# Gate logits through VectorE block transposes and a block-diagonal gate, for batches 3 to 7

## The chip, the cores and the metric

The kernel runs on one core of a Trainium2 chip. The metric is the device time of one execution in microseconds. All arrays are float32.

## The reference

An FFT filter over the sequence is followed by a mixture of experts in which every token goes to the one expert with the largest gate logit.

```python
# x: (8, 2496, 256); filter: (1249, 256) complex
X = np.fft.rfft(x, axis=1)
y = np.fft.irfft(X * (filt_r + 1j * filt_i)[None], n=2496, axis=1)   # (8, 2496, 256)

x = y.reshape(19968, 256)
logits = x @ w_gate                       # w_gate (256, 8)
expert_idx = np.argmax(logits, axis=1)
probs = np.exp(logits - logits.max(-1, keepdims=True))
probs /= probs.sum(-1, keepdims=True) + 1e-09
gate_w = probs[np.arange(N), expert_idx]
for e in range(8):                        # the tokens of each expert
    h = np.maximum(x[of_e] @ w1[e], 0.0)  # w1[e] (256, 1024)
    out[of_e] = gate_w[of_e, None] * (h @ w2[e])   # w2[e] (1024, 256)
```

## The kernel before

**The transform.** The length 2496 is 39 x 64, and the FFT is done as matmuls in four stages for each of the 8 batches. `stage_a` multiplies by a 39-point table, three blocks of 39 tokens at a time (117 partitions, TP). `stage_b` multiplies by a 64-point table, and VectorE applies the filter. `stage_c` is the 64-point inverse, and `stage_d` the 39-point inverse; its result `yo` holds y with tokens on the partitions (117 of them) and four columns of 256 features a tile. Between the stages the data goes through HBM (`zd`, `ud`). A batch has 22 such columns (NG), in six chunks (`CH`): five of four columns and one of two.

**The logits.** The gate needs features on the partitions. `turn_y` (L475) turns a chunk of y with TensorE transposes, 117x128 at a time, four for each pair of columns (L482), and copies the result from PSUM to `yt` with VectorE or ScalarE (`evac`, L234). `logits` (L488) takes four pairs at once and multiplies them by the gate matrix `wg`, padded to 32 columns: each pair writes 32 partitions of the PSUM tile `lt`, and so uses its own strip of 32 output columns of TensorE's array (L496). `turn_logits` (L502) copies `lt` to `ls`, transposes it back (L507) and stores it in `lg`, tokens on the partitions and 8 logits a token. A batch has three such groups, of 8, 8 and 6 columns.

**The routing.** `route` (L515), one call a group, finds the largest logit, the expert and the gate weight on VectorE. It ranks the tokens of each expert with two matmuls of the one-hot matrix `oe` by a triangle and by ones (`rk`, L554 and L555), which ScalarE copies to `pos` and `tot` (L557 to L559); VectorE scans and adds (L568 to L574) and writes `row`, the place of each token's row. GpSimd then appends the token's number and its gate weight `sd` to the rows of `yo` (L582, L586) and scatters them to HBM, one DMA for each column (L615).

**The experts.** The rows of each expert are read back in tiles of 512, 256 or 128, transposed on VectorE in blocks of 32x32 (`turn_x`, L748), and multiplied by w1 (L791 by a method with fewer products, or L832) and w2 (L849). The results are scattered to the output (L855).

**The order.** Nothing is ordered by the hardware's own choice: the program writes out each engine's queue by a small planner. `slot(k)` lists FFT steps with a due time within a slot, a cost, what they wait for and the stream they belong to: stage b and c of batch k, stage a of batch k+1, and stage d, logits and routing of batch k-1. The main loop takes the next step or, if a load is late (`late_in`), the first ready step of another stream (`other`), and mixes in expert steps by a credit. `now` is the planner's clock, `free` its belief of when VectorE ("v"), ScalarE ("s") and GpSimd ("p") are done. Routing runs as a generator in `side`, which can yield "wait" until the planner's clock has passed a due time. Tiles `yo` have 6 buffers (YB), `yt` 4.

Of the kernel before, what the change touches and what calls it, by code (L numbers as in the profile page):

```python
# [10 lines left out]
F32 = mybir.dt.float32  # L11
# [27 lines left out]
FT = F // P  # L39

# [13 lines left out]
def dft_tables():  # L54

    w = 2.0 * np.pi  # L60
    q = np.arange(N1)
    t = np.arange(N2)

    ta = np.zeros((NB, N1, NB, NS))
    td = np.zeros((NB, NS, NB, N1))
    for f in range(NF):
        ang = w * ((q * f) % N1) / N1
        for j in range(NB):
            ta[j, :, j, f] = np.cos(ang)
            td[j, f, j] = (2.0 if f else 1.0) / S * np.cos(ang)  # L70
            if f:
                ta[j, :, j, NF + f] = -np.sin(ang)
                td[j, NF + f, j] = -2.0 / S * np.sin(ang)

    ang = w * ((t[:, None] * t[None, :]) % N2) / N2
    c, sn = np.cos(ang), np.sin(ang)
    tb = np.block([[c, -sn], [sn, c]])
    tc = np.block([[c, sn], [-sn, c]])

    ids = np.zeros((NB, N1, NG))  # L80
    valid = np.zeros((NB, N1, NG))
    for j in range(NB):
        for i in range(len(range(j, N2, NB))):
            ids[j, :, i] = token(q, NB * i + j)
            valid[j, :, i] = 1.0


    sg = np.where(coefficients() <= S // 2, 1.0, -1.0)

    return {  # L90
        "ta": ta.reshape(TP, TK),
        "tb": tb,
        "tc": tc,
        "td": td.reshape(TK, TP),
        "sg": np.concatenate([sg[:, :NF // 2], sg[:, NF // 2:]]),
        "ids": ids.reshape(TP, NG),
        "valid": valid.reshape(TP, NG),
    }
# [22 lines left out]
def kernel(  # L121
# [52 lines left out]
    tau0 = perm.tile([1, 64], F32, name="tau0")  # L174
# [12 lines left out]
    tds = cst.tile([TK, TP], F32, name="tds")  # L187
# [4 lines left out]
    CT = 32  # L192
    wg = cst.tile([P, DH, CT], F32, name="wg")
    tri = cst.tile([TP, TP], F32, name="tri")
    ones = cst.tile([TP, P], F32, name="ones")
# [6 lines left out]
    vld = cst.tile([TP, NG], F32, name="vld")  # L202
    e_i = cst.tile([P, E], I32, name="e_i")
# [4 lines left out]
    tau_i = pro.tile([1, 64], I32, name="tau_i", bufs=1)  # L208
# [57 lines left out]
    def load_rest():  # L266
        nc.sync.dma_start(out=tds, in_=td)
        nc.vector.memset(wg, 0.0)
        nc.sync.dma_start(out=wg[:, :, :E], in_=moe_w_gate.rearrange("(i p) e -> p i e", p=P))
        nc.sync.dma_start(out=ids0, in_=ids)  # L270
        nc.sync.dma_start(out=vld, in_=valid)

    def make_constants():
        make_identity(nc, ident)
        nc.gpsimd.memset(ones, 1.0)
        nc.gpsimd.affine_select(
            out=tri, in_=ones[:, :TP], compare_op=ALU.is_gt, fill=0.0, base=0, pattern=[[1, TP]], channel_multiplier=-1
        )
        nc.gpsimd.memset(seg, 1.0)
        nc.gpsimd.memset(seg[:, :, 0:1], 0.0)  # L280
        nc.gpsimd.memset(tot, 0.0)
        nc.gpsimd.iota(prow, pattern=[[0, 1]], base=0, channel_multiplier=1)
        nc.gpsimd.iota(tau_i, pattern=[[1, 64]], base=0, channel_multiplier=0)
        nc.vector.tensor_copy(tau0, tau_i)
        nc.gpsimd.iota(e_i, pattern=[[1, E]], base=0, channel_multiplier=0)
        nc.vector.tensor_scalar(em8, in0=e_i, scalar1=-float(E), scalar2=None, op0=ALU.add)
        nc.vector.tensor_scalar(eoff, in0=e_i, scalar1=float(TE), scalar2=None, op0=ALU.mult)
        nc.vector.tensor_copy(cnt, eoff)
        nc.vector.tensor_copy(done, eoff[0:1, :])
        nc.vector.memset(one, 1.0)  # L290
# [106 lines left out]
    def stage_d(b, c):  # L397
        if c == 0:
            lgs[b] = sb.tile([TP, NG, E], F32, tag="lg", name="lg")
        i0, n = CH[c]  # L400
        held_y[0] += 1
        ui = outs.pop(("ui", c)) if b == 0 else ins.pop(("u", b, c))
        yo = outs["o", b, c] = sb.tile([P, 4, DR], F32, tag="y", name="yo", bufs=YB)[:TP]
        for j in range(0, n, 2):
            p = bank()
            if i0 + j + 2 < NG:
                mm(p[:TP, :], lhsT=tds, rhs=ui[:TK, j:j + 2, :], start=True, stop=True)
            else:

                for i, k in enumerate((TK, NS)):  # L410
                    mm(p[:TP, i * D:(i + 1) * D], lhsT=tds[:k, :], rhs=ui[:k, j + i, :], start=True, stop=True)
            evac(yo[:, j:j + 2, :D], p[:TP, :].rearrange("p (i d) -> p i d", i=2), 512)
# [63 lines left out]
    def turn_y(b, c):  # L476
        yo = outs["o", b, c]
        for j in range(0, CH[c][1], 2):
            pt = bank().rearrange("p (i q) -> p i q", i=4)
            for i in range(2):  # L480
                for dh in range(DH):
                    nc.tensor.transpose(  # L482
                        pt[:, 2 * i + dh, :TP], yo[:, j + i, dh * P:(dh + 1) * P], ident[:TP, :TP]
                    )
            yt = yts[b, c, j] = sb.tile([P, 4, TP], F32, tag="yt", name="yt", bufs=4)
            evac(yt, pt[:, :, :TP], 4 * TP)

    def logits(b, g):  # L488

        js = range(min(4, NG // 2 - 4 * g))  # L490
        w = len(js) * CT
        pair = [yts.pop((b, 2 * g + j // 2, 2 * (j % 2))).rearrange("p (i h) q -> p i h q", i=2) for j in js]
        lt = psr.tile([P, 2, E * NG], F32, tag="lt", name="lt")[:, :, :TP]
        for dh in range(DH):
            for j in js:
                mm(lt[j * CT:(j + 1) * CT], lhsT=wg[:, dh, :], rhs=pair[j][:, :, dh, :],  # L496
                   start=(dh == 0), stop=(dh == DH - 1))
        ls = sb.tile([P, 2, TP], F32, tag="ls", name="ls", bufs=1)
        evac(ls[:w], lt[:w], 2 * TP)
        outs["l", b] = (g, w, ls)  # L500

    def turn_logits(b):  # L502
# [5 lines left out]
        evac(lgs[b][:, 8 * g:8 * g + 2 * n, :].rearrange("p (j i) e -> p i j e", i=2),  # L508
# [5 lines left out]
    def route(b, c0, c1):  # L514
# [3 lines left out]
        lg = lgs[b][:, t0:t0 + w]  # L518
        sh3 = (TP, w, E)
        she = (TP, E, w)  # L520

        def small(name, *shape, dt=F32, tag=None):
            n = int(np.prod(shape))
            full = sb.tile([TP, WM * n // w], dt, tag=tag or name, name=name, bufs=1)[:, :n]
# [3 lines left out]
        mx = small("mx", w)  # L528
        nc.vector.tensor_reduce(mx, lg, axis=AX.X, op=ALU.max)
        oh = small("oh", w, E)  # L530
        ex = small("ex", w, E)
# [3 lines left out]
        nc.vector.tensor_tensor(oh, oh, em8[:TP, None, :].to_broadcast(sh3), op=ALU.mult)  # L535
        yield 2
        idx = small("idx", w)
        nc.vector.tensor_reduce(idx, oh, axis=AX.X, op=ALU.min)
        if t0 + w == NG:

            nc.vector.tensor_tensor(idx, idx, vld[:, t0:t0 + w], op=ALU.mult)
        oe = small("oe", E, w)
        nc.vector.tensor_tensor(
            oe, idx[:, None, :].to_broadcast(she), em8[:TP, :, None].to_broadcast(she), op=ALU.is_equal
# [7 lines left out]
        rk = bank()[:, :2 * E * w].rearrange("p (i n) -> p i n", i=2)  # L552
        oef = oe.rearrange("p e t -> p (e t)")
        mm(rk[:TP, 0, :E * w], lhsT=tri, rhs=oef, start=True, stop=True)  # L554
        mm(rk[:, 1, :E * w], lhsT=ones, rhs=oef, start=True, stop=True)  # L555
        pos = small("pos", E, w, tag="oh")
        nc.scalar.copy(out=pos.rearrange("p e t -> p (e t)"), in_=rk[:TP, 0, :E * w])  # L557
        nc.scalar.copy(out=tot[:, :, 1:w + 1], in_=rk[:, 1, :E * w].rearrange("p (e t) -> p e t", t=w))
        nc.scalar.copy(out=tot[:, :, 0], in_=cnt)  # L559
        free["s"] = max(free["s"], now[0]) + 1.2  # L560
        sd = small("sd", w)
# [7 lines left out]
        nc.vector.tensor_tensor(pos, pos, tot[:TP, :, :w], op=ALU.add)  # L569
        yield 2  # L570
        nc.vector.tensor_tensor(pos, pos, oe, op=ALU.mult)
        row = sb.tile([TP, WM], U32, tag="row", name="row", bufs=2)[:, :w]
        rowf = small("rowf", w)
        nc.vector.tensor_reduce(rowf, pos.rearrange("p e t -> p t e"), axis=AX.X, op=ALU.add)  # L574
        yield 2
        nc.vector.tensor_copy(row, rowf)
        nc.vector.tensor_copy(cnt, tot[:, :, w])
        yield 2
        for i, yo in enumerate(yos):
# [3 lines left out]
                yo.bitcast(I32)[:, :n, D:D + 8], in0=ids0[:, t0 + 4 * i:t0 + 4 * i + n, None].to_broadcast(sh8),  # L583
                scalar1=float(b * S), scalar2=None, op0=ALU.add,
            )
            nc.gpsimd.tensor_copy(yo[:, :n, D + 8:], sd[:, 4 * i:4 * i + n, None].to_broadcast(sh8))  # L586
# [42 lines left out]
    def tile_map(b, rows, n, last):  # L629
# [28 lines left out]
        ef = pools["moe"].tile([1, most], F32, tag="ef", name="ef", bufs=1)[:, :n]  # L658
# [17 lines left out]
        if not last:  # L676

            take = pools["moe"].tile([1, E], F32, name="take", bufs=1)
# [188 lines left out]
    def slot(k):  # L867
# [22 lines left out]
        if k > 0:  # L890
            for c in range(nch + 3):
# [3 lines left out]
                if c < nch:  # L895
                    steps.append((at, lambda c=c: stage_d(k - 1, c), ("u", k - 1, c) if k > 1 else "y", 0.43 * CH[c][1], "d"))
                if c >= 3 and c % 2:
# [29 lines left out]
    todo = [step[2] for step in STEPS if step[2] and step[2] != "y"]  # L927
# [132 lines left out]
    with tc.manual_schedule(  # L1060
# [11 lines left out]
        def ready(f):  # L1072
            return not halted(f) and (not f[2] or f[2] == "y" or f[2] in ins)

        def late_in(f):
            return f[2] and lands.get(f[2], 0.0) > now[0]
# [79 lines left out]
```

## Time and profile before

| | |
|---|---|
| time, median of 11 runs | 1524.35 us (1521.96 to 1527.63) |
| profiled execution: its own time | 1522.37 us |
| profiled execution: its span | 1520.7 us |
| mean granted TensorE clock | 0.993 |
| TensorE busy | 1464.7 us (96%) |
| VectorE busy | 752.5 us (49%) |
| ScalarE busy | 479.9 us (32%) |
| GpSimd busy | 696.2 us (46%) |
| DMA | 276.82 MB, mean 182 GB/s |

The span runs from the first instruction to the last; the execution's own time is 1.7 us longer. "PE" is TensorE's matmuls, "PEld" its weight loads, "DVE" VectorE, "ACT" ScalarE, "POOL" GpSimd and "SP" SyncE, whose queue issues most DMAs. A busy time is the union of an engine's instructions. Recorded durations of matmuls overlap, so the distance between the starts of two matmuls says what one costs. A line number such as L496 is that of the kernel before.

### The profile page before, as it was taken

What the parts mean: (1) busy time and instruction counts of PE and PEld (TensorE: products, weight loads), DVE (VectorE), ACT (ScalarE), POOL (GpSimd) and SP (SyncE); (2) the same over time, 40 slices, a digit from 0 to 9 for tenths busy, and PEclk for the clock granted to TensorE, in tenths of its full rate; (3) what the DMA queues carried; (4) which work ended last, traced back from release to release, by engine and by line L of the source; (5) the groups of instructions that cost most, each with busy time, mean ns of one, the idle gap of its engine ahead of it and who ended that gap; (6) DMA issues with size and microseconds to landing.
All of it is one profiled execution on the core that took longest, in us unless ns stands there. A gap on an engine that the chain in (4) does not pass through costs nothing. (4 is left out here: it accounts for less than half of the span.)

```text
span 1520.7 us, 23882 instructions
## 1 busy us (share of the span) xinstructions
PE 1464.7 (96%) x7202; PEld 1158.8 (76%) x7202; DVE 752.5 (49%) x1676; ACT 479.9 (32%) x993; POOL 696.2 (46%) x910
## 2 busy tenths in 40 slices
PE   7998897899999999999999999999999999999998
PEld 6543554776677876788778876888888889999997
DVE  4677574415755657455764545566535243440000
ACT  3443442233332333222232223222222222224332
POOL 3243344323635564446653545774546545741111
PEclk9999998999999999999999999999999999999999
DMA  9669897888695549735683554546565443455661
GB/s 241 190 181 304 244 320 233 231 221 238 204 284 167 184 128 259 193 98 160 168 223 96 155 147 131 162 139 188 149 175 188 147 139 103 122 186 171 187 184 40
DMA packets 215173, 276.82 MB, mean 182 GB/s; under 512 B 124227, under 2 KB 162508, under 8 KB 215045
## 3 DMA queue, kind: packets, MB, share of 16 engines
q1 hardware_dynamic: 195925, 231.94, 54.1%
q0 software_dynamic: 19120, 43.33, 8.4%
q8 instruction: 61, 1.00, 0.3%
q14 instruction: 67, 0.55, 0.1%
HBM read 195.19 MB, written 80.64 MB: 181 GB/s over the span
## 5 line engine op out<-in xcount | busy, mean ns | idle before, releaser
L849 PE MATMUL bank<-w2t,hT 128*128 128x256 f32 x1984 | 442.7, 380 | 4.4 <-ACT hT L799 3.5
L795 DVE TENSOR_TENSOR hT<-bank,hT 128x512 f32<-128x512 f32 (+1 forms) x504 | 299.7, 627 | 296.6 <-PE bank L791 202.3
L849 PEld LDWEIGHTS bank<-w2t,hT 128*128 128x128 f32 x1984 | 376.3, 191 | 69.8 <-issue 13.6
L855 POOL DMA_INDIRECT out_dram<-ys,ng x161 | 161.1, 1000 | 471.2 <-ACT ys L854 112.2
L799 ACT ACTIVATE hT<-hT 128x1024 f32<-128x1024 f32 (+1 forms) x144 | 132.3, 956 | 307.2 <-DVE hT L795 307.1
L615 POOL DMA_INDIRECT rows<-yo,row x176 | 176.8, 1004 | 72.4 <-issue 53.0
L854 ACT ACTIVATE ys<-bank,ng 128x256 f32<-128x256 f32 x137 | 65.0, 474 | 406.4 <-PE bank L849 315.5
L791 PE MATMUL bank<-xT,w1t 128*128 128x256 f32 (+1 forms) x864 | 192.0, 358 | 0.0
L791 PEld LDWEIGHTS bank<-xT,w1t 128*128 128x128 f32 x864 | 152.7, 192 | 25.2 <-issue 6.5
L791 PE MATMUL bank<-sums,wsum 128*128 128x256 f32 (+1 forms) x576 | 136.1, 359 | 0.1
L849 PE MATMUL bank<-w2s,hT 128*128 x592 | 132.6, 379 | 0.0
L748 DVE STREAM_TRANSPOSE xT<-xg 128x512 f32<-128x512 f32 (+2 forms) x126 | 57.5, 494 | 145.9 <-PE bank L832 113.0
L832 PE MATMUL bank<-xT,w1t 128*128 128x128 f32 (+1 forms) x864 | 124.3, 299 | 1.8 <-DVE xT L748 1.8
L832 PEld LDWEIGHTS bank<-xT,w1t 128*128 128x128 f32 x864 | 114.1, 191 | 12.9 <-issue 7.6
L849 PEld LDWEIGHTS bank<-w2s,hT 128*128 128x128 f32 x592 | 110.3, 190 | 13.8
L791 PEld LDWEIGHTS bank<-sums,wsum 128*128 128x128 f32 x576 | 101.5, 191 | 21.1 <-issue 9.7
L369 DVE TENSOR_TENSOR ys<-bank,ht 128x512 f32<-128x512 f32 x80 | 54.9, 686 | 74.1 <-PE bank L362 73.6
L348 PE MATMUL bank<-fin,tas 117*120 117x512 f32 x154 | 76.2, 614 | 8.2 <-DMA fin<-in_x_dram 7.3
L388 PE MATMUL bank<-ys,tcs 128*128 128x512 f32 x140 | 72.8, 603 | 8.0 <-DVE ys L378 5.4
L838 ACT ACTIVATE hT<-bank 128x128 f32<-128x128 f32 (+1 forms) x206 | 61.5, 299 | 48.5 <-PE bank L832 43.3
L766 POOL TENSOR_TENSOR wsum<-w1t 128x256 f32<-128x256 f32 x72 | 52.9, 734 | 50.5 <-PE bank L791 49.0
L362 PE MATMUL bank<-fin,tbs 128*128 128x512 f32 x140 | 71.8, 600 | 2.0 <-DMA fin<-zd 2.0
(143 smaller groups left out, 1612.2 us busy)
## 6 DMA issues: line engine op xcount, KB each, us to landing
w1t<-in_moe_w_dram SPq DMA_DIRECT2D x126, 512.0 KB
w2t<-in_moe_w_dram SPq DMA_DIRECT2D x68, 512.0 KB
fin<-in_x_dram SPq DMA_DIRECT2D x39, 512.0 KB
fin<-zd SPq DMA_DIRECT2D x70, 256.0 KB
ud<-uo SPq DMA_DIRECT2D x70, 256.0 KB
zd<-zo SPq DMA_DIRECT2D x35, 480.0 KB
fin<-ud SPq DMA_DIRECT2D x35, 480.0 KB
xg<-rows SPq DMA_DIRECT2D x112, 128.0 KB
```

The costliest lines, as they stand in the source:

```text
L348: mm(p[:TK, :], lhsT=tas, rhs=xt[:TP, j:j + 2, :], start=True, stop=True)
L362: mm(p, lhsT=tbs, rhs=zi[:, j:j + 2, :], start=True, stop=True)
L388: mm(p, lhsT=tcs, rhs=ys, start=True, stop=True)
L615: sc = nc.gpsimd.indirect_dma_start(out=rowsd, out_offset=bass.IndirectOffsetOnAxis(ap=at, axis=0), in_=what, in_offset=None,)
L791: mm(q[:, v], lhsT=left[:, v * P:(v + 1) * P], rhs=right, start=True, stop=True)
L795: nc.vector.tensor_tensor(o, q, a, op=ALU.add)
L799: nc.scalar.activation(o.rearrange("p v r c -> p v (r c)"), q.rearrange("p v r c -> p v (r c)"), AF.Relu)
L832: mm(p[:, :m], lhsT=w1t[2 * i + g][:, dh, fh, v * P:(v + 1) * P], rhs=xts[i][:, dh, :m], start=(dh == 0), stop=(dh == DH - 1))
L838: lambda: nc.scalar.activation(hT, p[:, :m], AF.Relu))
L849: mm(p[:, :D], lhsT=hs[i][k % 4 // 2][:, k // 4, k % 2, j * P:(j + 1) * P], rhs=w2, start=(k == 0), stop=(k == FT - 1))
L854: lambda: nc.scalar.activation(ys, p[:, :D], AF.Copy, scale=gate))
L855: nc.gpsimd.indirect_dma_start(out=out, out_offset=bass.IndirectOffsetOnAxis(ap=gis[i].bitcast(U32)[:, j, :1], axis=0), in_=ys, in_offset= ...
```

## The change

For batches 3 to 7 (`by_blocks`) the logits are made in another way; batches 0 to 2 keep theirs.

- `turn_block` turns y on VectorE: `nc.vector.transpose` turns each block of 32x32 of a pair of columns in place, SBUF to SBUF. `stage_d` writes 128 partitions instead of 117 for this (`tds` is padded), the last 11 zero.
- After such a turn a partition block of 32 holds 32 features of 32 tokens, and the four partition blocks hold four different sets of tokens. `wb` is the gate as a block-diagonal matrix: for each of eight sets of 32 features, four copies of the 32x8 gate, one for each partition block. `block_logits` multiplies, for each of four columns (q) and each of the eight sets (j), 32 moving columns by 32 columns of `wb`, adding over j in PSUM: 32 matmuls a chunk. One VectorE transpose by blocks puts the result into `lg`, where the tokens now stand in another order than in `yo`.
- `route` works on that order with 128 partitions and always 8 columns, with a mask for the padding. When places and gate weights are there (`rs`), 16 matmuls by strips of the identity bring them into the order of `yo`; VectorE and ScalarE copy them from PSUM to `row` and `gts`.
- In `slot`, turns and block logits have steps of their own; the logits are a stream "l" with a due time (`turned_at`) that is 4 us after the turn, or 2 us after VectorE is believed free.
- `ls` uses a buffer of `yt`; several small tiles share buffers.

```diff
+    by_block = np.zeros((4, CT, NG + 2))
+    by_block.reshape(P, NG + 2)[:TP, :NG] = valid.reshape(TP, NG)
+    by_block = by_block.reshape(4, CT, -1, 4).transpose(3, 1, 2, 0).reshape(P, -1)
...
-        "td": td.reshape(TK, TP),
+        "td": np.pad(td.reshape(TK, TP), ((0, 0), (0, P - TP))),
...
-    tri = cst.tile([TP, TP], F32, name="tri")
-    ones = cst.tile([TP, P], F32, name="ones")
+    wb = cst.tile([P, NJ, CT], F32, name="wb")
+    tri = cst.tile([P, P], F32, name="tri")
+    ones = cst.tile([P, P], F32, name="ones")
...
         nc.sync.dma_start(out=wg[:, :, :E], in_=moe_w_gate.rearrange("(i p) e -> p i e", p=P))
+        nc.vector.memset(wb, 0.0)
+        for i in range(4):
+            nc.sync.dma_start(out=wb[i * CT:(i + 1) * CT, :, i * E:(i + 1) * E], in_=moe_w_gate.rearrange("(j p) e -> p j e", p=CT))
...
     def turn_y(b, c):
         yo = outs["o", b, c]
+        if by_blocks(b):
+            for j in range(0, CH[c][1], 2):
+                yt = yts[b, c, j] = sb.tile([P, 2, D], F32, tag="yt", name="yt", bufs=4)
+                nc.vector.transpose(yt.rearrange("p i (j x) -> p i j x", x=CT),
+                                    yo[:, j:j + 2, :D].rearrange("p i (j x) -> p i j x", x=CT))
+                free["v"] = max(free["v"], now[0]) + 0.7
+            return
...
+    turned_at = {}
+
+    def turn_block(b, c):
+        turn_y(b, c)
+        turned_at["t", b, c] = max(now[0] + 4.0, free["v"] + 2.0)
+
+    def by_blocks(b):
+        return b >= 3
+
+    def block_logits(b, c):
+
+        lt = psr.tile([P, 2, E * NG], F32, tag="lt", name="lt")[:, 0, :CT]
+        n = CH[c][1]
+        pair = [yts.pop((b, c, j)) for j in range(0, n, 2)]
+        for j in range(NJ):
+            for q in range(4):
+                mm(lt[q * CT:(q + 1) * CT], lhsT=wb[:, j, :], rhs=pair[q % n // 2][:, q % 2, j * CT:(j + 1) * CT],
+                   start=(j == 0), stop=(j == NJ - 1))
+        nc.vector.transpose(lgs[b][:, 4 * c:4 * c + 4].rearrange("p i e -> p (i e)"), lt)
+        free["v"] = max(free["v"], now[0]) + 0.2
...
-        ls = sb.tile([P, 2, TP], F32, tag="ls", name="ls", bufs=1)
+        ls = sb.tile([P, 2, D], F32, tag="yt", name="ls", bufs=4)[:, :, :TP]
...
+        if by_blocks(b):
+            nc.vector.tensor_copy(cnt, tot[:, :, wide])
+            yield 2
+            due = free["v"] + 1.0
+            while now[0] < due:
+                yield "wait"
+            pr = bank()[:, :2 * wide].rearrange("p (g v c) -> p g v c", g=4, v=2)
+            rv = rs.rearrange("p v (c i) -> p i v c", i=4)
+            for g in range(4):
+                for i in range(4):
+                    mm(pr[i * CT:(i + 1) * CT, g], lhsT=ident[:, g * CT:(g + 1) * CT], rhs=rv[:, i], start=True, stop=True)
+            sd = sb.tile([P, WM], F32, tag="gts", name="gts", bufs=2)[:, :wide]
+            nc.vector.tensor_copy(row.rearrange("p (c g) -> p g c", g=4), pr[:, :, 0])
+            nc.scalar.copy(out=sd.rearrange("p (c g) -> p g c", g=4), in_=pr[:, :, 1])
+            free["s"] = max(free["s"], now[0]) + 0.3
+        else:
+            nc.vector.tensor_copy(row[:TP], rowf)
+            nc.vector.tensor_copy(cnt, tot[:, :, wide])
...
+                if by_blocks(k - 1):
+                    if 1 <= c <= nch:
+                        steps.append((at + 0.03, lambda c=c: turn_block(k - 1, c - 1), None, 0.0, "d"))
+                        steps.append((at + 0.031, lambda c=c: block_logits(k - 1, c - 1), ("t", k - 1, c - 1), 0.6, "l"))
+                        if c % 2 == 0:
+                            steps.append((at + 0.032, lambda c=c: sides.append(route(k - 1, c - 2, c)), None, 0.0, "l"))
+                    continue
```

## The prediction

> **What bounds the kernel now.** I read the shares of busy time first, then the same by stage, then the costliest groups of TensorE with the shapes kept apart, then single stretches of the timeline.
>
> ```profile
> PE 1464.7 (96%) x7202; PEld 1158.8 (76%) x7202; DVE 752.5 (49%) x1676; ACT 479.9 (32%) x993; POOL 696.2 (46%) x910
> ```
>
> The share is an average, so the next view is busy time in four stretches (PE, PEld, DVE, ACT, POOL, then granted clock, DMA share, GB/s). The logits of batches 3 to 7 lie between 390 and 1010 us.
>
> ```profile
> 0.00:310.00 310.00, 270.14 (x1164) 166.01 (x1165) 184.52 (x461) 117.30 (x255) 122.01 (x157) 0.97 0.82 241
> ...
> 390.00:1010.00 620.00, 610.75 (x2812) 477.36 (x2811) 361.86 (x764) 185.46 (x339) 332.02 (x434) 1.00 0.61 170
> 1010.00:1520.70 510.70, 503.99 (x2876) 458.31 (x2874) 174.73 (x393) 148.57 (x336) 216.87 (x287) 1.00 0.50 152
> ```
>
> In the stage of the change TensorE works 610.75 of 620 us at full clock, VectorE 58% and ScalarE 30% of it. After 1010 us only expert matmuls are left, at the same density. Expert tiles fill every gap that a batch leaves, so TensorE time saved in batches 3 to 7 reaches the end nearly one for one; so does any added. The waits of TensorE in that stage are few:
>
> ```profile
> PE lt L496 <- DVE yt L234: 2.6, 1, 2.6
> PE bank L482 <- DVE yo L234: 2.2, 1, 2.2
> PE bank L554 <- DVE oe L543: 1.7, 2, 1.1
> ```
>
> So the sum is one over TensorE's time, and a matmul's price is the distance between starts, not its duration: durations (380 ns for 256 columns) overlap their successors.
>
> **What goes.** Per batch of 3 to 7: 44 transposes of y (L482), three blocks of logits (L496), three turns of logits (L507). The timeline (start, length) gives one of each, with what follows it:
>
> ```profile
> 653.68 0.81 PE L849 MATMUL bank<-w2t,hT 128*128 128x256 f32 x3
> 654.42 1.00 PE L496 MATMUL lt<-yt,wg 128*32 128x234 f32 x16
> 655.36 0.92 PE L849 MATMUL bank<-w2t,hT 128*128 128x256 f32 x3
> ...
> 594.04 0.97 PE L482 MATMUL bank<-ident,yo 117*128 117x117 f32 x8
> 594.84 1.04 PE L849 MATMUL bank<-w2t,hT 128*128 128x256 f32 x4
> ...
> 677.84 0.38 PE L507 MATMUL bank<-ident,ls 128*117 128x128 f32 x2
> 678.06 0.60 PE L791 MATMUL bank<-xT,wsum 128*128 128x256 f32 x2
> ```
>
> - Transposes: 594.84 - 594.04 = 0.80 for eight, 0.1 each: 4.46 per batch with 0.01 lost after each of the six runs.
> - A block of logits: start to next start 0.94. A stream of 256 columns has starts 0.216 apart, and the block begins 0.09 later than that after its predecessor; the three matmuls after it last 0.92 instead of 0.81, another 0.10. So 1.13, three times 3.39. The 16 passes (a float32 matmul is recorded as two: 22 of L496 a batch, 352 records in all) run four at a time on four strips of 32 output columns, in four rounds of 0.20, so 1.13 - 0.80 = 0.33 is the fixed price of going into strips and back.
> - Turn of logits: 0.22, three times 0.65.
>
> Together 8.5 us per batch, 42.5 us for five. (The groups' busy sums, 43.8 + 26.9 + 9.0 over eight batches, make 10.0 per batch; they count drains that lie under the next work.)
>
> **What comes on TensorE.** Per batch six blocks of 32 matmuls 32x32 (64 passes), and three permutations of 16 matmuls with 4 columns (32 passes). In rounds of four strips: 6 x 16 + 3 x 8 = 120, and nine visits to the strips instead of three. Visits: 9 x 0.33 = 2.97. Open is the price p of a round, since no matmul in the trace is this small:
>
> - From below, by the nearest row, L496. Four strips start within 20 ns:
>
> ```profile
> 654.42 0.41 PE L496 MATMUL lt<-yt,wg 128*32 128x234 f32 x4
> ```
>
>   Each lasts 387 ns and the four together 0.41, so they start 6.7 ns apart and issue needs 27 ns a round. Streaming: 0.20 for 234 columns is 0.85 ns a column, 27 for 32. Loading 32 weight columns: first-round matmuls last 387 ns, later ones 361, so the exposed load is 26 ns, and the four loads run side by side (the fourth matmul is no longer than the first). Where load and stream are equally long (L832, 128 columns) starts lie 0.112 apart against 0.107 of streaming, so they overlap at some 5 ns extra. p = 27 + 5 = 32 ns. Feeding: by the trace's records of PE's sequencer, set against the instruction order, two semaphore waits with 16 loads and matmuls between them are 139 ns apart at best, with 24 between them 168: 3.6 ns an instruction, 29 ns a round of eight.
> - From above: load and stream one after the other, 27 + 27 + 2 = 56 ns.
> - By the rule against this change: the Trainium skill, "TensorE: Matmul & The Clock Gate", section "Wait — 56ns, not 53.3ns?", says that starts of matmuls never come closer than about 25 ns however small they are. As a limit over all strips that is 100 ns a round. The 6.7 ns above speak against reading it so; as a limit within one strip it is met by 27. But four starts are a burst, and no run here shows sixteen small rounds in a row, nor rounds adding to the same 32 PSUM columns every 30 ns.
>
> I take 32, the value that L496 and L832 give. New work per batch: 2.97 + 120 x 0.032 = 6.8, against 8.5: **-1.7 per batch, -8.5 in all**. The balance is zero at p = 46 ns; by the upper end, 56, the five batches lose 6 us, by the rule's reading (100) 32 us.
>
> Around a block the sequencer's queue is drained about as fast as it is filled, and each recorded semaphore wait costs the sequencer 125 ns. I charge 0.05 for each of the 45 visits: **+2**. Bounds: 0, and 0.15 each (7 us).
>
> **Waits.** The 2.6 us before L496 and the 2.2 before L482 have no instruction left to strike. But VectorE's delay behind them remains and can hold its next reader: I count half, -2.5. New: block_logits waits for VectorE's transposes, but the planner holds it back 4 us after they are queued; behind a late one stand all expert matmuls. The permutation waits for rowf and cnt, and in the new instruction order at least four matmuls of 512 columns (8 x 0.43 = 3.4 us) separate it from the rank matmuls. The chain between is 0.3 of drain, ScalarE's pos, tot, tot (0.20 + 0.22 + 0.22), VectorE's scan, add, multiply, reduce (0.42 + 0.32 + 0.34 + 0.26): 2.1 us without queueing, so most are in time. 15 permutations at 0.1 and 30 blocks at 0.02 make +2. Net **-0.5** (range -5 to +5).
>
> **Off the path.** VectorE gains 11 transposes of 128x512 per batch (685 ns, the xT row of this stage), six of logits (0.2), two masks (0.3) and loses about four yt copies (0.64): +6.7 us per batch, from 58% to 64% of the stage. ScalarE loses about 4. Their cover is TensorE; only a VectorE late by more than the 4 us would show. tds and tri with 128 instead of 117 columns are loads under matmuls: 0.01 a batch. The wider third route runs the same scatters. In the start, one memset and four DMAs are queued on SyncE before ids, vld and three stores of z:
>
> ```profile
> 35.75 0.40 SPq L269 DMA_DIRECT2D wg<-in_moe_w_gate_dram  x1
> 36.20 0.42 SPq L270 DMA_DIRECT2D ids<-in_ids_dram  x1
> 36.67 0.37 SPq L271 DMA_DIRECT2D vld<-in_valid_dram  x1
> 37.14 8.82 SPq L307 DMA_DIRECT2D zd<-zo  x3
> ```
>
> Four issues are 1.7 us; the three stores behind them take 8.8 us waiting for zo. I cost them at nothing; if that cover is gone, 1.7, because z loads are late next. ls now shares yt's four buffers in batches 0 to 2; its reader stands before the reuse in program order: nothing.
>
> **Sum.** -8.5 + 2 - 0.5 = -7. The profiled execution took 1522.4 (span 1520.7), 2 below the median of the runs, 1524.35; on that median: 1517.4.
>
> **Rivals.**
> A, as summed: 1513 to 1521, chance 0.45.
> B, the gain is spent at the edges: queue drain and late permutations cost each of the 45 visits 0.15 more, +7, so 1524 (1521 to 1527). For: nine visits a batch instead of three, six or more of them waiting for a shorter chain than before. Against: all waits of TensorE in the stage come to 9 us today. 0.19.
> C, slower: rounds of 32 columns cost over 46 ns (43 with the 2 us of edges), because a load is not hidden under so short a stream, or because of a floor per start or for adding into PSUM. At 56: +7.4, 1532; at 100: +34, 1558. For: the rule above, and that a batch has 480 small passes in place of 94. Against: the spacing, overlap and feeding worked out above. 0.28, of which 0.10 for the far end.
> D, the removed waits stay away, edges cost nothing: -8.5 - 5 = -13.5, 1511. 0.08.
> That the change does not do what it says is excluded by the instruction order: 30 blocks of 32 and 15 permutations stand there, and no L482 or L507 in batches 3 to 7.
>
> **How the numbers follow.** This kernel's measurement tells 0.2%, 3 us, from no change. Faster: A nearly whole, D, a little of B: 0.55. Same: most of B, a little of A: 0.14. Slower: C and the rest of B: 0.31. The range of 1509 to 1535 holds A, B, D and the near end of C, and leaves out C's far end and edges. Faster cases alone: 1510 to 1521.
>
> **What would show it.** Right: in the new timeline a block of 64 lasts about 0.84 from start to next start, edges included, a permutation 0.6; TensorE's busy sum falls by some 10 us or more; waits on rs and yt stay under 4 us together. Wrong: rounds over 46 ns, gaps of several hundred ns before the permutations, or a first stage (0 to 310 us) that ends later.

## The result and the profile after

| | before | after |
|---|---|---|
| time, median | 1523.34 us (30 runs, 1520.12 to 1527.63) | 1508.45 us (8 runs, 1505.03 to 1512.94) |
| ratio | | 0.9901, 95% interval 0.9888 to 0.9913 |
| profiled execution: own time, span | 1522.37, 1520.7 us | 1508.67, 1506.9 us |
| mean granted clock | 0.993 | 0.992 |

The change took 14.9 us off where 7.0 were forecast; the direction was right, and the time lies just below the range that was given (1509). First the shares of busy time of after:

```profile
PE 1456.9 (97%) x9132; PEld 1153.8 (77%) x9132; DVE 769.4 (51%) x1731; ACT 465.6 (31%) x964; POOL 696.9 (46%) x910
```

TensorE has 1930 instructions more and 7.8 us of busy time less; GpSimd has the same 910. By stage (PE, PEld, DVE, ACT, POOL, granted clock, DMA share, GB/s):

```profile
0.00:310.00 310.00, 271.28 (x1162) 167.62 (x1163) 184.95 (x462) 117.17 (x254) 121.85 (x157) 0.97 0.83 242
...
390.00:1010.00 620.00, 615.47 (x4574) 481.27 (x4573) 395.62 (x881) 175.60 (x320) 337.05 (x439) 1.00 0.64 176
1010.00:1506.90 496.90, 490.22 (x2812) 446.19 (x2810) 153.41 (x322) 145.51 (x332) 207.96 (x275) 1.00 0.50 149
```

The start, where five things were added, is no later (271.28 against 270.14 us of TensorE in 310). In the stage of the change TensorE is idle for 4.5 us instead of 9.25, and the last stage is 13.8 us shorter at the same density: expert matmuls filled what the logits left, as the prediction had it. Its waits between 310 and 1120 us:

```profile
PE bank L848 <- DVE hT L852: 2.6, 1, 2.6
PE bank L356 <- DMA fin<-in_x_dram: 1.1, 1, 1.1
PE bank L627 <- DVE rs L615: 0.4, 1, 0.4
PE bank L595 <- DVE oe L584: 0.3, 1, 0.3
```

The waits on `yt` and `yo` that led the list of before are gone, and the new readers, L520 on `yt` and L627 on `rs`, wait 0.4 us together. But two waits are new, 2.6 us of an expert matmul (L848) on VectorE and 1.1 us on a load. The timeline has one block and one permutation, each with what follows (start, length):

```profile
596.48 0.76 PE L520 MATMUL lt<-yt,wb 128*32 128x32 f32 x64
597.17 1.12 PE L370 MATMUL bank<-fin,tbs 128*128 128x512 f32 x2
...
669.14 0.44 PE L627 MATMUL bank<-rs,ident 128*32 128x4 f32 x32
669.51 0.92 PE L848 MATMUL bank<-xT,w1t 128*128 128x256 f32 x3
```

A block takes 0.69 from start to next start, and with the 0.09 ahead of it and the 0.10 behind, 0.88; the forecast was 0.84. A permutation takes 0.37 and with its edges 0.56; 0.6 was forecast.

So the parts cost what they should: 30 blocks and 15 permutations make 34.8 us. The surplus is seen when the old blocks are looked at one by one rather than by the view of waits. Two of the fifteen of batches 3 to 7 in the trace of before:

```profile
552.31 0.59 PE L496 MATMUL lt<-yt,wg 128*32 128x234 f32 x4
553.11 0.98 PE L496 MATMUL lt<-yt,wg 128*32 128x234 f32 x8 [0.21 <-ACT yt L234]
554.02 1.35 PE L791 MATMUL bank<-xT,w1t 128*128 128x256 f32 x5
...
880.27 0.59 PE L496 MATMUL lt<-yt,wg 128*32 128x234 f32 x4
883.46 1.48 PE L496 MATMUL lt<-yt,wg 128*32 128x234 f32 x8 [2.59 <-DVE yt L234]
884.87 1.65 PE L791 MATMUL bank<-sums,wsum 128*128 128x256 f32 x3
```

They take 554.02 - 552.31 = 1.71 and 884.87 - 880.27 = 4.60 us; a third, at 397.7, takes 2.16. The other twelve take 0.93. All three are the last group of a batch, with three pairs of columns, and TensorE reaches the third pair before its copy to `yt` is done. Those at 397.7 and 552.31 stand directly behind the transposes L482 of their own columns; at 880.27 VectorE still has a row of small routing instructions (880.04 to 882.8) ahead of the copy.

The three hold 5.7 us more than undisturbed ones. Of this the view of waits lists 3.5 (3.7 with an earlier batch): by the starts, the third strip is 1.24, 0.79 and 3.17 us late, 5.2 together, but the view counts a gap only from the modelled end of the passes of the other two strips, 0.59 us into the block. The other 0.5 is clock. Behind the longest wait the trace has TensorE at half its clock for 3.41 us, from 883.79 on, in the block and in the expert matmuls after it: three of them take 1.65 us above, where 0.81 is undisturbed.

The next line is that stretch of before in the form of the views by stage (granted clock 0.96), and the last one the other wait that went:

```profile
858.00:897.00 39.00, 36.41 (x167) 28.68 (x166) 21.05 (x42) 10.31 (x20) 17.29 (x23) 0.96 0.41 113
...
918.48 1.22 PE L482 MATMUL bank<-ident,yo 117*128 117x117 f32 x8 [2.24 <-DVE yo L234]
```

### The profile page after: what moved, and what is told of

Its sections match the earlier page's. It is cut to its first block, busy times and chain, and to the rows that moved or that the text cites. A ratio compares the mean times of both kernels' runs of the same rounds, so it can differ in the third digit from the quotient of the medians.

```text
span 1506.9 us, 27754 instructions
## 1 busy us (share of the span) xinstructions
PE 1456.9 (97%) x9132; PEld 1153.8 (77%) x9132; DVE 769.4 (51%) x1731; ACT 465.6 (31%) x964; POOL 696.9 (46%) x910
## 5 line engine op out<-in xcount | busy, mean ns | idle before, releaser
L848 PE MATMUL bank<-xT,w1t 128*128 128x256 f32 (+1 forms) x864 | 191.4, 358 | 0.0
L848 PEld LDWEIGHTS bank<-xT,w1t 128*128 128x128 f32 x864 | 152.7, 191 | 21.0 <-issue 3.2
L848 PE MATMUL bank<-sums,wsum 128*128 128x256 f32 (+1 forms) x576 | 135.1, 357 | 2.6 <-DVE hT L852 2.6
L906 PEld LDWEIGHTS bank<-w2s,hT 128*128 128x128 f32 x592 | 110.3, 190 | 13.8
L848 PEld LDWEIGHTS bank<-sums,wsum 128*128 128x128 f32 x576 | 101.4, 190 | 22.4 <-issue 10.7
```

What stands on the lines that cost most here:

```text
L848: mm(q[:, v], lhsT=left[:, v * P:(v + 1) * P], rhs=right, start=True, stop=True)
L906: mm(p[:, :D], lhsT=hs[i][k % 4 // 2][:, k // 4, k % 2, j * P:(j + 1) * P], rhs=w2, start=(k == 0), stop=(k == FT - 1))
```

## The experiments

They ran on three other chips than the comparison above (its chip is called the first chip from here on). There the kernel before takes not 1523 but 1553 to 1563 us. What that came from turned out to be the larger part of the study. "Theory" in an expectation is what would be so if one cause were the right one; each is stated where it first stands.

**A due time alone.** The old path is kept, and a block of the old logits in batches 3 to 7 is held back until 4 us after its last turn is queued:

```diff
     def turn_y(b, c):
...
+        turned_at["t", b, c] = now[0] + 4.0
...
-  steps.append((at + 0.01, lambda c=c: logits(k - 1, (c - 3) // 2), None, 0.9, "d"))
+  steps.append((at + 0.01, lambda c=c: logits(k - 1, (c - 3) // 2), ("t", k - 1, min(c - 2, nch - 1)) if k > 3 else None, 0.9, "d"))
...
-            return f[2] and lands.get(f[2], 0.0) > now[0]
+            return f[2] and (lands.get(f[2], 0.0) > now[0] or turned_at.get(f[2], 0.0) > now[0])
```

> The old path (TensorE transposes, four pairs a group) for all batches; only the planner's part of the change is taken over: in batches 3 to 7 a group of logits is held back until 4 us after its last turn of y was queued. Theory 1 (the gain beyond TensorE's own work is the wait of the old logits for the copy of y just turned: start to start, the 15 blocks L496 of batches 3 to 7 hold 5.7 us more than 15 undisturbed ones): 4 to 8 us faster than the kernel before, and no block L496 longer than 1.0 us from start to next start. Theory 2 (the gain beyond the work comes from what the shorter path lets the planner do with the expert tiles, not from these waits): within 2 us of the kernel before, the waits only move to other instructions.

Measured: 1531.5 against 1557.55 us, ratio 0.9843 (0.9814 to 0.9871). That is 26 us, more than any theory had, and with no new path at all.

**No due time.** The new path with `turned_at["t", b, c] = now[0]`.

> The changed kernel without the due time: block_logits may be queued as soon as its turn is. Theory 1: the waits come back on TensorE, since two VectorE transposes of 0.7 us and what is queued before them lie between turn and logits: 0.7 to 2 us for each of 30 blocks, so 20 to 60 us slower than the changed kernel, 1530 to 1570. Theory 2: the due time is of little weight, within 5 us of the changed kernel.

Measured: 1663.69 us, ratio 1.0668 (1.0630 to 1.0706). Its waits of TensorE (total us, times, longest):

```profile
PE lt L520 <- DVE yt L489: 58.0, 36, 6.9
PE lt L520 <- issue: 23.8, 41, 2.8
```

The due time is no ornament: without it the blocks wait 58 us for VectorE (in c_after below, with it, that line is absent). The second line was not expected. "Issue" is time in which TensorE waits for nothing that the profile shows.

**Every block twice** (`for j in [*range(NJ), *range(NJ)]`; the second time overwrites the first, so the logits stay as they are).

> The changed kernel with every block of logits computed twice in the same visit to the strips (the second time overwrites the first): 30 x 16 more rounds of four strips. Theory 1 (TensorE's time in this stage reaches the end one for one, a round costs 33 ns): 16 us slower than the changed kernel, about 1524. A rival in which a good part of TensorE's time in this stage is covered by idle time: under 8 us.

Measured: 1600.67 us, ratio 1.0279 (1.0248 to 1.0310): 77 us above the 1524 of theory 1, and again

```profile
PE lt L520 <- issue: 41.5, 64, 2.2
```

**Two chunks a visit.** 15 visits to the strips in place of 30, with 128 passes each.

```diff
-        lt = psr.tile([P, 2, E * NG], F32, tag="lt", name="lt")[:, 0, :CT]
+        both = psr.tile([P, 2, E * NG], F32, tag="lt", name="lt")
+        for h in range(2):
+            lt = both[:, h, :CT]
```

> The changed kernel with the logits of two chunks in one visit to the strips (15 visits of 128 passes instead of 30 of 64), the turns in the same stream as the logits so that four yt buffers suffice. Theory 1: 15 visits less at 0.33 us, 5 us faster than the changed kernel (1503 to 1506), if no wait grows. Rival: the later turns and the longer block give it back in waits of TensorE or in later routing, 1507 to 1512.

Measured: 1548.1 us, ratio 0.9944 (0.9916 to 0.9973), with 17.0 us of "issue" before its blocks.

After these four it was plain that the blocks behave differently here. So the two kernels themselves were run on another chip of this kind.

> The kernel before unchanged, for its trace on the chip of this call. In the call before, it took 1557.55 us (median of 11) where it took 1523.34 on other chips. Theory 3 (the chip of that call supplies TensorE's instructions more slowly, so short matmuls starve): if this is such a chip, holes of 0.3 us and more stand inside L496 or L482 without a wait; if it is a chip like the first, 1520 to 1528 and no such holes.

> The changed kernel unchanged, beside the kernel before on one chip. On a chip like the first: ratio 0.990, holes inside L520 of 0.2 us at most. On a chip like that of the call before (theory 3): holes of 0.65 us inside L520, and a ratio that tells how much of the gain they take; theory 1 without them would still say 0.990.

Measured: before 1553.31 (median of its runs beside the others; the profiled one 1561.04), after 1570.1, ratio **1.0093** (1.0063 to 1.0124). The change that gains 1% on the first chip loses 1% on this one. From start to start the 1920 passes of the blocks take 52.1 us in c_after and 22.6 us in after. The 29 us are holes, most of them of 0.6 to 0.7 or 1.33 us, with one to six passes and as many loads between them.

> The old path with the due time for the logits of batches 3 to 7, again, on the chip of the two controls. Theory 1: 4 to 8 us faster than the kernel before (ratio 0.995 to 0.997) with the blocks L499 undisturbed. Theory 2: 0.999 to 1.002.

Measured: 1532.78 us, ratio 0.9847 (0.9817 to 0.9877).

**One batch more by blocks** (`b >= 2`).

> The changed kernel with batch 2 on the new path too (its begin_route is put in the stream of the logits, so that it stays behind them). Theory 1: TensorE is full from 310 us on, and batch 2 is turned there: a fifth of what five batches gave, 2 to 3 us faster than the changed kernel. Rival: VectorE (up to 79% in slices of this stage) or the wider row buffers hold it back, 0 to 4 us slower.

Measured: 1593.36 us, ratio 1.0245 (1.0211 to 1.0279), 28.1 us of "issue": 23 us slower than c_after beside it, with 41 us of holes instead of 29. The other half of the 23 was not traced.

Then three kernels were run again, and it was tried whether the length of a stretch of short passes makes the holes.

> The changed kernel again, beside the kernel before. On the chips of the first comparison it took 14.9 us less than the kernel before (ratio 0.990), on the chip of c_after 1.009 of it, with 28.8 us of holes inside its 30 blocks. Theory S (the holes decide, and they belong to the chip): where the kernel before comes out near 1523 us the ratio is 0.990 and the blocks hold under 3 us of holes; where it comes out near 1553 us, the ratio is 1.005 to 1.012 and the blocks hold 20 to 35 us. Theory N (the holes came from something else in that run): the ratio doesn't go with the time of the kernel before.

Measured: 1571.17 against 1555.77 us, ratio 1.0102 (1.0079 to 1.0125), 37 us of holes. Theory S held (with 2 us more of holes than its range).

> The old path of logits, only held back until 4 us behind its last turn. Where the kernel before comes out near 1523 us: if the waits in the old blocks (5.7 us inside the blocks, 2.4 us behind one) made up the larger part of what the change brought, this alone gains 6 to 9 us (ratio 0.994 to 0.996), and the new path is 6 to 9 us faster still; if the shorter TensorE work made it, under 3 us. Where it comes out near 1553 us: 0.984 again, as twice before.

Measured: 1532.33 us, ratio 0.9853 (0.9827 to 0.9879).

**Blocks in halves.** Two visits of 32 passes with other matmuls between them:

```diff
+            turned_at["t", b, c, 1] = now[0] + 1.2
...
-        for j in range(NJ):
+        for j in range(h * NJ // 2, (h + 1) * NJ // 2):
```

> Each block of 64 passes is cut into two of 32 with other matmuls of at least 1.2 us between them. The holes on the chip of c_after lay from the 29th to 45th pass of a block on. Theory Q (a stretch of short passes uses up what is queued ahead of TensorE, and the long ones between refill it): on such a chip the holes fall from 28.8 us to under 8 us, and though 30 more visits cost 0.19 us each (5.7 us), it is 12 to 20 us faster than the changed kernel there. Theory T (the supply of instructions is slow at certain times, whatever runs): the holes stay at 20 to 30 us, and it is 5 us slower than the changed kernel. On a chip with few holes both say 5 to 6 us slower than the changed kernel.

Measured: 1579.37 us, ratio 1.0160 (1.0130 to 1.0190), 8 us slower than c_after2 beside it. Its holes add up to 19.5 us, and in one half they begin at the third pass. So theory Q fell: against the 37 us beside it the holes halve but do not vanish, and they need no long stretch. That they come at certain times (theory T) was left.

> Two chunks' blocks in one visit: 15 visits to TensorE's column strips instead of 30, the same 1920 passes. Where the kernel before comes out near 1523 us: 15 visits less at 0.19 us each are 2.9 us; it is 1 to 4 us faster than the changed kernel unless the longer stretch of 128 short passes opens holes. Where it comes out near 1553 us: 0.994, as before, with 20 us of holes.

Measured: 1546.01 us, ratio 0.9936 (0.9915 to 0.9957), 24 us of holes, as expected. It is 25 us faster than c_after2 beside it; 13 of them are fewer holes, the rest was not traced.

**What runs at these times.** The timelines of TensorE and of GpSimd in c_after2, in the same stretch:

```profile
705.87 0.96 PE L520 MATMUL lt<-yt,wb 128*32 128x32 f32 x50
707.29 0.27 PE L520 MATMUL lt<-yt,wb 128*32 128x32 f32 x4 [0.47 <-issue]
708.02 0.28 PE L520 MATMUL lt<-yt,wb 128*32 128x32 f32 x5 [0.47 <-issue]
708.75 0.28 PE L520 MATMUL lt<-yt,wb 128*32 128x32 f32 x5 [0.45 <-issue]
709.49 1.02 PE L396 MATMUL bank<-ys,tcs 128*128 128x512 f32 x2 [0.46 <-issue]
```

```profile
706.02 1.00 POOL L672 DMA_INDIRECT rows<-yo,row  x1 [0.19 <-POOL yo L643]
707.33 0.98 POOL L672 DMA_INDIRECT rows<-yo,row  x1 [0.30 <-issue]
708.62 0.98 POOL L672 DMA_INDIRECT rows<-yo,row  x1 [0.30 <-issue]
```

The block starts at 705.87, the scatters at 706.02; 50 passes run, then four or five at a time. Counted over all blocks, by whether GpSimd spent over 0.1 us of the block in an indirect DMA:

| | blocks with one | of these with holes | holes, us | blocks without | holes, us |
|---|---|---|---|---|---|
| c_after | 12 | 11 | 28.8 | 18 | 0.0 |
| c_after2 | 14 | 14 | 37.2 | 16 | 0.0 |
| after (first chip) | 15 | 7, of 0.2 us each | 1.4 | 15 | 0.0 |

(A hole is a distance between starts of over 0.1 us; the 36.7 us of an expectation below are the 37.2, counted a little differently.) In these three no block without an indirect DMA has a hole, and in c_after and c_after2 79 of the 83 holes overlap one. In e3, e4 and e5, with more passes at a time or in all, one or two blocks without have some, 1.0 to 3.1 us in all. (In e2 twelve have, where the blocks also wait for VectorE.) That is a coincidence in time and not yet a cause, so the indirect DMAs were then taken away, from both kernels and from the old path with its due time. They became plain ones on the same engine, to rows known ahead; eight indirect ones behind 1137 us, which pad the rows of the experts, stay. These kernels leave the sorting by expert out of the result, so they tell about time alone. The cuts, shortened:

```diff
-        sc = nc.gpsimd.indirect_dma_start(out=rowsd, out_offset=bass.IndirectOffsetOnAxis(ap=at, axis=0), in_=what, in_offset=None)
+            r0, m = placed[0], what.shape[0]
+            placed[0] += m
+            sc = nc.gpsimd.dma_start(out=rowsd[r0:r0 + m, :], in_=what)
...
-        rows = rowsd[bass.ds(r0, n * P), :]
+        r1 = min(sum(m for m, _ in TILES[:i]) * P, N - n * P)
+        rows = rowsd[r1:r1 + n * P, :]
...
-        nc.gpsimd.indirect_dma_start(out=out, ...)
+        nc.gpsimd.dma_start(out=out[r0:r0 + P, :], in_=ys)
```

> The changed kernel with POOL's indirect DMAs (rows<-yo,row and out_dram<-ys,ng) turned into plain DMAs on POOL's queue to fixed rows, the reads of rows at fixed places too: the experts get their rows in the order of the tokens, which leaves the sorting by expert out of the result. In c_after2, 14 of 30 blocks ran while POOL was at an indirect DMA, and these 14 hold all 36.7 us of holes; the 16 others hold none. Theory P (POOL's indirect DMAs starve TensorE's stream of short passes on these chips): under 3 us of holes in the blocks, and against x2 a ratio near 0.990, as in the first comparison: 10 to 18 us faster than x2. Theory T (the supply is slow at these times for another reason, such as the load on the DMA engines): 20 to 37 us of holes stay, and it is 10 to 20 us slower than x2.

> The kernel before with the same edit (plain DMAs for POOL's indirect ones; the sorting of rows by expert is left out of the result). Its own time on these chips stands some 32 us above the 1523 us of the first ones. Theory P: most of that goes too, 20 to 35 us faster than the kernel before. Theory T: within 8 us of the kernel before.

> The old path of logits, only held back until 4 us behind its last turn, with the same edit (plain DMAs; the sorting by expert is left out). Between x2 and x1 it splits what the change is worth without the holes: if the waits in the old blocks made up the larger part of the 14.9 us, it is 6 to 10 us faster than x2 and x1 is 5 to 8 us faster than it; if the shorter TensorE work did, it is under 3 us faster than x2. If it is as fast as x1 or faster, the new path gains nothing over a due time alone.

| beside the kernel before at 1563.05 us | time, us | ratio to it |
|---|---|---|
| x2, before without indirect DMAs | 1519.43 | 0.9717 (0.9689 to 0.9744) |
| x3, old path with the due time, without | 1511.54 | 0.9664 (0.9642 to 0.9686) |
| x1, after without | 1506.40 | 0.9628 (0.9603 to 0.9653) |

Theory P (the indirect DMAs starve TensorE) held, and by more than it said. x1 against x2 is 0.9909 (0.9875 to 0.9943, worked out from the means of the five times of each); by medians it is 13.0 us faster, the first chip's result again. The groups by shape, c_after2 and then x1:

```profile
L520 PE MATMUL lt<-yt,wb 128*32 128x32 f32 x1920 | 34.1, 200 | 27.8 <-issue 27.5
```

```profile
L520 PE MATMUL lt<-yt,wb 128*32 128x32 f32 x1920 | 22.9, 199 | 0.0
```

All 30 blocks of x1 take 0.69 us. The plain DMAs move as much through the same queue of GpSimd. Queue lines of c_after2 and of x1 (packets, MB, share of the 16 engines):

```profile
q0 software_dynamic: 19120, 43.33, 8.1%
```

```profile
q0 software_dynamic: 16432, 43.97, 8.6%
```

So it is not the bytes on that queue. What is gone is the indirect instruction, which held GpSimd about 1.0 us where a plain one holds it 0.54, and with it one more thing: SyncE's reads of the rows no longer take their addresses from registers. Those reads are not what makes the holes: six of the 14 blocks with holes in c_after2, the one above among them, have neither such a read nor SyncE's register instructions in them, and two of the 16 without holes have such a read. The two lines of GpSimd:

```profile
L672 POOL DMA_INDIRECT rows<-yo,row x176 | 177.8, 1010 | 64.6 <-issue 45.3 <-DVE row L633 5.1 <-POOL yo L643 4.5
```

```profile
L684 POOL DMA_DIRECT2D rows<-yo x176 | 93.3, 540 | 9.1 <-issue 4.0 <-POOL yo L643 3.7 <-DMA out_dram<-ys 1.0
```

VectorE stands as well. In c_before its list of waits has lines that the first chip's before has not (there "issue" is 0.3 us in all) and that x2 has not either. TensorE waits longer for VectorE there (its rank matmuls L554 on `oe` for 10.9 us between 310 and 1120, on the first chip for 1.9):

```profile
DVE hT L795 <- issue: 14.6, 7, 9.1
DVE xT L748 <- issue: 6.9, 2, 6.5
DVE ys L369 <- issue: 5.0, 4, 3.1
```

Seven indirect DMAs run in the longest of these, 9.1 us. This fits that the kernel before itself loses 43.6 us to x2, but the 43.6 were not added up from waits: between 390 and 1010 us TensorE is idle for 22.4 us in c_before against 9.25 on the first chip, at a granted clock of 0.98 against 1.00.

**Blocks moved away from scatters,** in the complete kernel, by the planner's belief of GpSimd (and with the routing of a batch moved into stream "l", since its last block can now be late):

```diff
+        def scattering(key):
+            return key in turned_at and free["p"] + 0.5 > now[0] < turned_at[key] + 6.0
...
-            return f[2] and (lands.get(f[2], 0.0) > now[0] or turned_at.get(f[2], 0.0) > now[0])
+            return f[2] and (lands.get(f[2], 0.0) > now[0] or turned_at.get(f[2], 0.0) > now[0] or scattering(f[2]))
```

> The changed kernel, complete, with one more condition on a block of logits: it also waits, for up to 6 us of the planner's time, until the planner has no indirect DMA on POOL. Theory P: fewer blocks meet one (14 of 30 in c_after2), and the holes fall in proportion to the blocks that still do, at about 2.6 us each: with 6 of 30, 16 us of holes and a ratio near 0.997 where the kernel before comes out near 1553 us. Theory T: holes of 28 to 37 us and 1.01 stay.

Measured: 1602.39 us, ratio 1.0247 (1.0214 to 1.0280). Not separated: 13 of 30 blocks still meet an indirect DMA, all 13 with holes, 34.8 us in all (2.7 each, where theory P had 2.6), against none in the other 17. There are new waits on top, 12.2 us of L848 on GpSimd's `wsum` and 4.3 of the permutations on VectorE; that the later routing made them is not shown. As a remedy it failed, and as a test of the cause it is one more count of the same kind.

## Why the prediction was right and wrong

**Right: the bound.** TensorE's time saved in batches 3 to 7 reached the end: the last stage, with expert matmuls alone, is 13.8 us shorter.

**Right: the price of a round.** 32 ns was taken against 56 and against the rule's 100. In an undisturbed block of after, four starts 6.7 ns apart come every 32 ns at first, and later pairs of starts every 16.7 ns, 33 ns a round of four, sixteen rounds on end. Rival C died there. The rule of the Trainium skill ("TensorE: Matmul & The Clock Gate", "Wait — 56ns, not 53.3ns?") holds at most for one strip: matmuls on different strips start 6.7 ns apart here.

**Right: the edges.** +2 was charged. Nine blocks of after are 0.07 to 0.25 us longer than the other 21, 1.8 us in all. Blocks and permutations came out 0.04 above and 0.04 below the forecast. So work and edges are 34.8 + 1.8 - 42.5 = -5.9 us, where the sum had -8.5 + 2 = -6.5. The reason given for the edges is weaker: 125 ns is the commonest distance between two semaphore waits in the records of PE's sequencer (39 times), while the record of one lasts 51; that a wait costs 125 is not shown.

**Right: waits of the new path.** Under 4 us on `rs` and `yt` was the condition; it is 0.4. Also right was what gave that: e2, without the due time, waits 58.0.

**Wrong: the waits that were removed.** The step that failed is "The 2.6 us before L496 and the 2.2 before L482 have no instruction left to strike ... I count half, -2.5", with +2 for new waits: net -0.5. Of the 13.8 us between the two profiled spans, work and edges leave some 8 for waits. Read from the traces, it comes to that:

- The three blocks L496 were held for 5.2 us, not 2.6, and another 2.4 lay before L482, up to 918 us.
- Half clock for 3.41 us behind the longest wait is 1.7 us of TensorE by estimate. After has no such stretch between 310 and 1500 us. That the wait brought it is not shown: the 2.6 us wait of after and the one before L482 are not followed by one.
- Smaller waits of before shrank or went: L554 on `oe` from 1.7 to 0.3, L388 and L849 with 1.8 together.
- New are 2.6 us of an expert matmul (L848) on VectorE, which was late with a row of small instructions as in before, 1.1 on a load and 0.4 on `rs`: 4.1 us that came in.

So what came back was about what the prediction had (half of 4.8, and 2: 4.4); the mis-sized part is what went, 4.8 in the sum and some 12 in the traces. As a check, TensorE is idle for 4.7 us less in the stage (9.25 to 4.5), and the wait under modelled ends (5.2 - 3.5) and the clock are 1.7 each: 8.1 us net, where the sum had 0.5. The clock and the smaller waits may be luck of the order; no forecast had them. The sign "TensorE's busy sum falls by some 10 us or more" was missed too (7.8).

The chip splits the gain in a like way where both kernels run without indirect DMAs. x3 against x2 is the due time alone: 7.9 us by medians, 7.1 by means (ratio 0.9953, 0.9924 to 0.9983). Its trace has fourteen of the fifteen blocks at 0.93 us, the last at 1.51, new waits of 2.1 us on VectorE before its expert matmuls (L802), and none of the two stretches of half clock, 3.4 us each, that x2 has there. x1 against x3 is the new path's work: 5.1 us by medians, 6.8 by means (0.9955, 0.9928 to 0.9982), where the sum had 6.5. The intervals are wide, some 4 us to each side, so that the two shares are about equal is all that they tell; but that the waits are worth at least 2.6 us there and not 0.5 is shown. Rival D (-13.5) was the nearest, and it had 0.08; it was near in part by luck, since it had 2.6 us more for the work than was measured and some 3 less for the waits.

**Missed: what the gain hangs on.** Neither the sum nor a rival had GpSimd's indirect DMAs. The 30 new blocks are a dense stream of instructions (64 passes and 64 loads in 0.69 us), and where indirect DMAs open holes in it, they lose 29 to 37 us and the sign turns: 1.009 and 1.010. On such a chip the old path with a due time is the best complete kernel that was run, 0.984 to 0.985 of the kernel before in three comparisons, 37 to 39 us below the changed kernel in the two where both ran side by side. It was not run on the first chip; there x3 against x1 suggests that it would stay some 5 to 7 us behind the changed kernel. Why it gains 20 to 26 us on the other chips, and 7 to 8 without indirect DMAs, was not traced.

**Open.** Why the chips differ, or whether it is the chip at all and not a state that it was in; one of them was used twice and was the same both times (1557.55 and 1555.77 us for the kernel before). On the first chip the same indirect DMAs take as long on GpSimd (980 to 990 ns by the median, on both kinds) and leave holes of 0.2 us at most. And what exactly they hold up: the 16 KB instruction packets take 1.0 to 1.1 us by the median in before, after, c_before and c_after2, so it is not visible there.

## What to carry to other kernels

Before counting a wait as the view of waits shows it, compare each instance of the group with an undisturbed one: what lies above is the wait, however it is cut up, and look at the granted clock behind it. A consumer that is ordered directly behind its producer's copy is worth a due time before it is worth a new algorithm; in x3 that gave about half of the gain for six changed lines. And a change that replaces few long instructions by many short ones depends on how fast they come: look for what else runs at those times, GpSimd's indirect DMAs first, and measure on more than one chip.

## What the hardware showed that was not expected

- While GpSimd is in an indirect DMA (about 1.0 us each, 345 of them), TensorE may get only one to six short matmuls with their loads in each 0.7 us, or in 1.35 us at times, and VectorE stood up to 9.1 us. With plain DMAs of about the same bytes from the same engine all of it is gone (holes 37.2 to 0 us, the kernel before 43.6 us faster). The extent depends on the chip: the blocks lose 1.8 us on the first, 29 to 37 us on those of the experiments.
- Clock goes with the holes: the mean granted clock is 0.975 in c_after2 and 0.993 in x1. The trace of c_after2 has stretches of 3.4 and 6.8 us at half the rate, among others from 387.7, 428.6, 609.5, 824.6 and 872.3 us on, each in a block with holes or just behind it.
- Sixteen rounds of four matmuls of 32 columns on the four strips run at 32 to 34 ns a round, adding to the same PSUM columns; going into strips and back costs some 0.30 us (permutations) to 0.35 us (blocks) a visit.
